# Expert 0's late tokens through DRAM, casts that give way, shorter routing, fillers at the seam and a new order in an attention + mixture-of-experts kernel

## The chip, the cores and the metric

One core of a Trainium2 chip runs one program. The metric is device microseconds of that core; the kernel before takes 403.33 us (median of 3 runs, 403.32 to 403.79).

## The reference

q, k, v, a_re and a_im are (4 batches, 8 heads, 768 steps, 48 dims). The first part is a gated linear recurrence with a complex decay, whose real part is read out by q:

```python
mag = np.sqrt(a_re * a_re + a_im * a_im)
scale = np.minimum(mag, 0.999) / (mag + 1e-06)
ar, ai = a_re * scale, a_im * scale
for t in range(S):
    S_re, S_im = (ar[t] * S_re - ai[t] * S_im + outer(k[t], v[t]),
                  ar[t] * S_im + ai[t] * S_re)
    y[t] = q[t] @ S_re
```

The second part takes y as x, 3072 tokens of 384. A token whose score `x @ w_skip` is not above 0 is copied. Any other token goes to the one of 8 experts that has the largest logit in `x @ w_gate`, and

```python
out = x + softmax_weight * (relu(x @ w1[e]) @ w2[e])      # w1: 384 x 1024, w2: 1024 x 384
```

All of it is float32.

## The kernel before, in words

**Units.** The attention is cut into 24 units: 6 chunks of 128 time steps (NCH) times 4 batches (B); unit u is chunk u // 4 of batch u % 4 and holds all 8 heads. `gates` computes a unit's decay (logs, exponentials, angles; ScalarE and VectorE, and two TensorE sums over time, `pt` and `pl`), `ready` loads q and k, multiplies them with the decay (`w`), transposes them on TensorE (`tp`, L437) and copies them out of PSUM on ScalarE (`wT`, L446). `unit` does the attention: `pa` (L478) and `py` (L520, L523) on TensorE work in 64-column halves, `yT` (L528, ScalarE) copies the result, and `px` (L537) turns it to token rows with the gate logits beside them. `lg` (L549, VectorE) sums the logits, `xa` (L553, ScalarE) copies the rows. Gates run in batches of units (STARTS), since ScalarE's tables for exponentials and for sines are loaded in turn.

**Routing.** For chunks 0 to 4, `route` works on four units at once: maximum of the logits, expert number, one-hot `oh`, a rank among the tokens of that expert (`rank`, bf16 matmuls), the softmax weight, a slot number. Then four indirect DMAs (`place`, L586, GpSimd queue) scatter the rows to a DRAM buffer `xs`, with 224 slots (CAP) for each expert. For the last chunk, `route1` (chain rt5_b and its second half re b) does the same unit by unit, b = 0 to 3.

**Expert 0 at the seam.** Expert 0 does not wait for the last four units' rows to go through DRAM. `early` (L583, SyncE queue) reads its slots once chunk 4's rows have landed, and for each of the last four units `spread` (L679) makes a 128 x 224 selection matrix `ohx`; the pieces `ga` (L883) then gather: 12 ordinary matmuls for each unit with its `ohx`, and 12 for the early rows with an identity matrix, in the order unit 20, 21, 22, early, 23, all summed in one PSUM tile. Copies of it (`xh`, L909, and the rest `xl`, L913) feed expert 0's first layer.

**Experts.** For each expert, `xg` (L891) loads its rows, `tx` (L903) transposes them, `ph` (L927) is layer 1 and `po` (L948 to L950) layer 2, each product in three float32r matmuls of high and low parts; `hh` and `hl` split the hidden values, `og` adds the weighted result, and `sc` scatters the rows to the output. The weights come in 7 pieces for each expert: `wd` (L843, SyncE queue), then a cast to the high part `wh` (L850, ScalarE, 0.8 to 1.1 us) and the low part `wl` (L855, VectorE, 0.9 to 1.2 us). Experts 0 and 1 are loaded and cast while the attention still runs.

**The order.** Every piece is handed to a planner (`Plan`) with an engine, an estimated time, a due time, what it needs and which buffers it takes. The planner runs a list schedule on these estimates: the engine that can start first takes, of the pieces that can start at that moment, the one with the smallest due time. SHIFT moves the due times of a kind of piece. The instructions are then issued on each engine in this order, and each engine works strictly through its own queue. So a piece whose inputs are later than the planner thought holds up everything behind it. Where the planner sees TensorE idle before the first `py`, it puts filler matmuls (`idle`, L755).

## Time and profile before

| what | us |
|---|---|
| median of 3 runs | 403.33 |
| profiled execution | 405.78 |
| its span, first to last instruction | 404.1 |
| TensorE busy in the span | 382.1 (95%) |
| VectorE busy | 318.0 (79%) |
| ScalarE busy | 278.8 (69%) |
| GpSimd busy | 68.8 (17%) |

The span is what the trace shows; the profiled execution adds 1.7 us around it. Busy time says what an engine had in flight, not that it was at its peak, and fillers count as busy. "Clock 1.00" is TensorE at its full 2.4 GHz, 0.50 is 1.2 GHz.

### The profile page before, as it was taken

The numbers are of one execution on the slowest core, as the hardware profiler recorded it, in microseconds if no ns is written. First come the engines' busy times: TensorE is split into PE (matmuls) and PEld (weight loads), VectorE is DVE, ScalarE is ACT, GpSimd is POOL, SyncE is SP. The second block draws the span as 40 slices with busy tenths as digits, with TensorE's granted clock in tenths as the row PEclk, the third lists the DMA queues.
The fourth block names the chain that finished last, engine by engine and source line by source line (L and its number), as shares of the span: only waits on it lengthen the run. The fifth ranks groups of instructions, "written<-read, shape, count | busy, mean of one in ns | idle before, by whom it ended". The sixth has DMA issues, their size and how long they took to land. (4 is left out here: it accounts for less than half of the span.)

```text
span 404.1 us, 9935 instructions
## 1 busy us (share of the span) xinstructions
PE 382.1 (95%) x3768; PEld 345.5 (86%) x3768; DVE 318.0 (79%) x728; ACT 278.8 (69%) x546; POOL 68.8 (17%) x102
## 2 busy tenths in 40 slices
PE   7888999999999999999998998899999999999992
PEld 7577788789888789889877988799999999999992
DVE  5679999999999999999978879858765777757220
ACT  5897989999998999698785574445454755546110
POOL 9100000034005100400540033102111110110101
PEclk9999999999999999999999899899999999999997
DMA  9958979789798688454625785596777868771001
GB/s 157 194 100 156 186 120 285 178 194 196 136 159 207 133 173 186 108 109 117 128 93 142 193 233 172 177 317 215 224 227 222 235 191 236 226 222 38 27 2 34
DMA packets 160758, 67.15 MB, mean 166 GB/s; under 512 B 142310, under 2 KB 156295, under 8 KB 160704
## 3 DMA queue, kind: packets, MB, share of 16 engines
q1 hardware_dynamic: 158144, 61.81, 64.8%
q0 software_dynamic: 2560, 4.63, 3.5%
q8 instruction: 32, 0.52, 0.5%
q14 instruction: 22, 0.18, 0.2%
HBM read 54.24 MB, written 14.98 MB: 171 GB/s over the span
## 5 line engine op out<-in xcount | busy, mean ns | idle before, releaser
L850 ACT CAST h<-r 128x768 fp32r<-128x768 f32 (+1 forms) x56 | 50.9, 928 | 36.3 <-PE po L950 20.4
L586 POOL DMA_INDIRECT xs<-xa,sl x24 | 35.8, 1493 | 206.7 <-ACT ain L261 75.4
L855 DVE TENSOR_TENSOR l<-r,h 128x768 fp32r<-128x768 f32 (+1 forms) x56 | 59.2, 1070 | 11.0 <-ACT h L850 11.0
L446 ACT COPY wT<-tp 96x512 f32<-96x512 f32 x92 | 50.3, 582 | 7.1 <-PE tp L437 7.1
L437 PE MATMUL tp<-ident,w 128*96 128x128 f32 x384 | 53.2, 278 | 1.9 <-DVE w L429 0.6
L927 PE MATMUL ph<-xh,h 128*128 128x224 f32 x192 | 53.7, 283 | 1.2 <-ACT xh L909 0.9
L927 PE MATMUL ph<-xh,l 128*128 128x224 f32 x192 | 52.9, 279 | 0.0
L927 PE MATMUL ph<-xl,h 128*128 128x224 f32 x192 | 50.6, 277 | 0.0
L437 PEld LDWEIGHTS tp<-ident,w 128*96 128x96 f32 x384 | 41.6, 128 | 8.3 <-issue 2.4
L933 ACT ACTIVATE hh<-ph 128x224 fp32r<-128x224 f32 x64 | 22.8, 359 | 34.8 <-PE ph L927 34.7
L429 DVE TENSOR_TENSOR w<-qk,cs 128x768 f32<-128x768 f32 x48 | 44.5, 949 | 0.2
L948 PE MATMUL po<-h,hh 128*112 128x384 f32 x128 | 43.5, 340 | 0.0
L950 PE MATMUL po<-h,hl 128*112 128x384 f32 x128 | 43.1, 337 | 0.0
L949 PE MATMUL po<-l,hh 128*112 128x384 f32 x128 | 43.1, 337 | 0.0
L478 PE MATMUL pa<-wT,wT 96*64 96x128 f32 (+1 forms) x768 | 38.2, 250 | 2.4 <-ACT wT L446 1.9
L927 PEld LDWEIGHTS ph<-xh,h 128*128 128x128 f32 x192 | 37.5, 195 | 1.8 <-ACT xh L909 1.0
L927 PEld LDWEIGHTS ph<-xh,l 128*128 128x128 f32 x192 | 37.7, 196 | 0.0
L520 PE MATMUL py<-at,vt 128*64 128x128 f32 x192 | 36.5, 279 | 1.1 <-DVE at L485 0.7
L478 PEld LDWEIGHTS pa<-wT,wT 96*64 96x64 f32 x768 | 33.7, 137 | 4.0 <-ACT wT L446 2.3
L937 DVE SCALAR_TENSOR_TENSOR hl<-ph,hh 128x224 fp32r<-128x224 f32 x64 | 23.6, 385 | 17.1 <-ACT hh L933 17.1
L520 PE MATMUL py<-at,vs 128*64 128x128 f32 x192 | 36.5, 279 | 0.0
L927 PEld LDWEIGHTS ph<-xl,h 128*128 128x128 f32 x192 | 36.1, 195 | 0.0
(170 smaller groups left out, 852.2 us busy)
## 6 DMA issues: line engine op xcount, KB each, us to landing
r<-in_moe_w_dram SPq DMA_DIRECT2D x24, 512.0 KB, 5.0
r<-in_moe_w_dram SPq DMA_DIRECT2D x32, 384.0 KB, 5.5
ain<-in_a_re_dram SPq DMA_DIRECT2D x24, 192.0 KB, 3.5
ain<-in_a_im_dram SPq DMA_DIRECT2D x24, 192.0 KB, 4.5
qk<-in_q_dram SPq DMA_DIRECT2D x24, 192.0 KB, 4.1
qk<-in_k_dram SPq DMA_DIRECT2D x24, 192.0 KB, 4.1
vt<-in_v_dram SPq DMA_DIRECT2D x24, 192.0 KB, 4.1
out_dram<-xa SPq DMA_DIRECT2D x5, 768.0 KB, 4.1
```

Source lines behind the costliest of these rows:

```text
L429: V.tensor_tensor(n, X["qk", u][:, k].unsqueeze(2).to_broadcast([128, H, 2, D]), X["cs", c][:, b], ALU.mult)
L437: nc.tensor.transpose(tp[:, h], n[:, hh * 4 + h].rearrange("p k d -> p (k d)"), self.ident)
L446: (V.tensor_copy if onV else A.copy)(X["wT", u, k][:, hh * 4:hh * 4 + 4], X["tp", u, k, hh])
L478: PE.matmul(pa[p, i, t0:], k[:, h, ts], q[:, h, t0:], start=True, stop=True)
L520: PE.matmul(py[j * 64:j * 64 + 64, hp], vs[:, hp] if j else vt[:, 2 * hp], at[:, 2 * hp + j], start=True, stop=(c == 0))
L586: self.nc.gpsimd.indirect_dma_start(out=self.xsv[c * B + b], out_offset=bass.IndirectOffsetOnAxis(ap=sl, axis=0), in_=xa[:, b], in_offset= ...
L850: nc.scalar.copy(X["W", e, n][0][:, ks], X["raw", e, i])
L855: nc.vector.tensor_tensor(lo[:, ks], X["raw", e, i], hi[:, ks], ALU.subtract)
L927: PE.matmul(ph, w[:, k, ks(j)], x[:, k], start=(i == 0), stop=(i == len(terms) - 1))
L948: PE.matmul(po, hh[:, j, ts(t)], w2h[:, j], start=(j == 0), stop=False)
L949: PE.matmul(po, hh[:, j, ts(t)], w2l[:, j], start=False, stop=False)
L950: PE.matmul(po, hl[:, j, ts(t)], w2h[:, j], start=False, stop=(j == NF - 1))
```

## The change

- The pieces `ga` of units 20 and 21 are gone (EARLY = 2). Their rows for expert 0 go through `xs` like all others; `early` now reads after the placements of these two units, and only units 22 and 23 get an `ohx`. The order is early, 22, 23, and the early rows are turned in transpose mode.
- The placements of units 22 and 23 wait for `early`.
- In the planner, where the piece chosen is a weight cast, any other piece of that engine that can start less than 0.71 us later (LOOK) goes first. The last cast of expert 1 comes after expert 0's input (HOLD).
- Routing: one step makes the expert number and the skip mark together (a skipped token gets an expert number of -8192, which puts its slot out of bounds); the small sum constant 1e-9 lives in a ninth column of a shared tile; the overflow mark is written straight to `todo`. `route` goes from 19 + 3 VectorE instructions to 13 + 2, `route1` from 10 + 9 pieces to 8 + 5 (units 20, 21), 10 + 5 (22) or 9 + 5 (23). The experts' regions of `xs` are in reverse order, with expert 0's last.
- Fillers are also put in where the planner sees TensorE idle between the last `yT` and the first `ph`. The first `ph` comes after the last decay factors (`f3`) and after the last rank sum.
- New planner constants: batches of gates (the last starts at unit 22, not 21), leads, SHIFT, a cost for each turn between half-width and full-width matmuls (TURN), and FINE, which moves single pieces; many `po` pieces are moved 10 to 20 units later, that is behind any other piece that can start.

```diff
-STARTS = [0, 3, 7, 11, 14, 18, 21]
-AHEAD, TRIG, READY, PULL = 3.0, 2.98, 1.66, 2.83
+STARTS = [0, 3, 7, 11, 14, 18, 22]
+AHEAD, TRIG, READY, PULL = 3.0, 3.08, 1.72, 2.49
-WAFTER, WGAP, CHECK = 5.0, 2.02, 3
-FETCH = 2.75
+WAFTER, WGAP, CHECK = 4.65, -0.13, 3
+FETCH = 2.87
+EARLY, HOLD, LOOK = 2, 6, 0.71
+FINE = {
...
+}
-LEADS = {0: 6.57, 1: 7.36, 2: 2.93, 3: 1.62, 4: 2.78, 5: 0.77, 6: 1.2, 7: 4.57}
+LEADS = {0: 7.24, 1: 6.22, 2: 3.18, 3: 1.87, 4: 3.38, 5: 0.58, 6: 0.38, 7: 3.19}
...
+            if key[0] in ("wh", "wl"):
+                s, at, key = min([x for x in l if x[0] < s + LOOK and x[2][0] not in ("wh", "wl")] or [(s, at, key)], key=lambda x: (x[0], str(x[2])))
-            if e == "P" and n > 0 and ("py", 0, 0) not in end:
+            if e == "P" and n > 0 and (("py", 0, 0) not in end or ("yT", B * NCH - 1) in end and ("ph", 0, 0) not in end):
...
-        self.nc.sync.dma_start(self.xe, self.xs[0:CAP, 0:DM].rearrange("(t p) d -> p t d", p=HALF))
+        self.nc.sync.dma_start(self.xe, self.xs[E * CAP:(E + 1) * CAP, 0:DM].rearrange("(t p) d -> p t d", p=HALF))
...
         steps = [
             ("V", 0.15, first),
-            ("V", 0.22, lambda: V.scalar_tensor_tensor(R["cand"], R["L"], R["mx"], iota, ALU.is_equal, ALU.mult)),
-            ("V", 0.15, lambda: V.tensor_scalar(R["act"], R["lg"][:, E:], 0.0, None, ALU.is_gt)),
+            ("V", 0.22, lambda: V.scalar_tensor_tensor(R["cand"][:, 0:E], R["L"], R["mx"], iota, ALU.is_equal, ALU.mult)),
+            ("V", 0.15, lambda: V.tensor_scalar(R["cand"][:, E:], R["lg"][:, E:], 0.0, -OFF, ALU.is_le, ALU.mult)),
             ("V", 0.15, lambda: V.tensor_reduce(R["am"], R["cand"], AX.X, ALU.min)),
-            ("V", 0.22, lambda: V.scalar_tensor_tensor(R["oh"], iota, R["am"], R["act"].to_broadcast([128, E]), ALU.is_equal, ALU.mult)),
+            ("V", 0.16, lambda: V.tensor_scalar(R["oh"], iota, R["am"], None, ALU.is_equal)),
             ("P", 0.15, rank),
...
-            ("V", 0.22, lambda: V.scalar_tensor_tensor(R["val"], R["oh"][:, 0:1], -BIG, R["pr"][:, 0:1], ALU.mult, ALU.add)),
+            ("V", 0.22, lambda: V.scalar_tensor_tensor(R["val"][:, 0:1], R["oh"][:, 0:1], -BIG, R["pr"][:, 0:1], ALU.mult, ALU.add)),
             ("V", 0.35, spread),
+        ] * (b >= EARLY) + [
+            ("V", 0.22, lambda: V.tensor_tensor_reduce(R["val"], R["oh"], R["pr"], 1.0, 0.0, ALU.mult, ALU.add, accum_out=R["rk"])),
+        ] + [("V", 0.15, sums)] * (b < B - 1)
...
-            self.plan.add(("early", 0), "S1", 1.1, at, [(f"rt{c - 1}", 19 + B)], take=[("xa", "early")])(self.early)
+            self.plan.add(("early", 0), "S1", 1.1, at + EARLY, [(f"rt{c - 1}", 14 + B)] + [(f"re{k}", 5) for k in range(EARLY)], take=[("xa", "early")])(self.early)
...
+            ("G1", 0.3, lambda: self.place(c, b, R["sl"], R["xa"]), ("xa", c * B + b), *[("early", 0)] * (b >= EARLY)),
...
-        for b in (0, 1, 2, -1, 3):
+        gas = [-1] + list(range(EARLY, B))
+        for i, b in enumerate(gas):
...
-                        PE.matmul(pts(0, t)[:, k], l, r, start=(b == 0 and k == 0), stop=True, skip_group_check=True)
+                        PE.matmul(pts(0, t)[:, k], l, r, start=(b < 0 and k == 0), stop=True, is_transpose=b < 0, skip_group_check=True)
...
-                     [(None, ("ph", e, j - 1))] * (j > 0) + [("at", u, 1), ("yT", u)] * (e == 0),
+                     [(None, ("ph", e, j - 1))] * (j > 0) + [("at", u, 1), ("yT", u), ("f3", c), (f"rt{c}_{B - 1}", 10)] * (e == 0),
```

## Rows read from the trace of the kernel before

**Rows 1.** Stretches of the span: us, each engine busy, TensorE clock, DMA share, GB/s.
```profile
0.00:36.00 36.00, 29.59 (x224) 25.40 (x224) 24.23 (x50) 27.89 (x52) 10.47 (x49) 1.00 0.94 149
36.00:218.00 182.00, 178.27 (x2100) 150.85 (x2102) 174.57 (x398) 165.15 (x331) 30.39 (x21) 1.00 0.73 156
...
246.00:258.37 12.37, 9.66 (x85) 8.70 (x85) 11.00 (x60) 5.11 (x12) 5.21 (x4) 1.00 0.56 159
258.37:396.90 138.53, 138.16 (x1003) 136.69 (x1003) 85.05 (x151) 63.71 (x123) 17.78 (x23) 0.99 0.59 179
396.90:404.10 7.20, 0.00 (x0) 0.00 (x0) 0.62 (x1) 0.00 (x0) 0.94 (x1) 0.68 0.08 23
```

**Rows 2.** Two shorter stretches, same columns.
```profile
221.00:227.00 6.00, 6.00 (x52) 5.51 (x54) 5.17 (x10) 3.36 (x7) 0.00 (x0) 0.72 0.73 179
259.00:264.00 5.00, 5.00 (x33) 5.00 (x31) 4.59 (x11) 1.96 (x5) 0.00 (x0) 0.66 0.65 194
```

**Rows 3.** TensorE timeline: start, us, line, out<-in, count, idle before and releaser.
```profile
218.73 0.88 PE L478 MATMUL pa<-wT,wT 96*64 96x64 f32 x16
220.95 0.93 PE L478 MATMUL pa<-wT,wT 96*64 96x128 f32 x16 [1.34 <-ACT wT L446]
```

**Rows 4.** ScalarE timeline, the same place.
```profile
219.37 1.04 ACT L850 CAST h<-r 128x1024 fp32r<-128x1024 f32 x1 [1.82 <-DMA r<-in_moe_w_dram]
220.32 0.57 ACT L446 COPY wT<-tp 96x512 f32<-96x512 f32 x1
```

**Rows 5.** TensorE timeline, from the last attention piece to the first expert.
```profile
245.61 0.39 PE L523 MATMUL py<-wT,st 96*64 96x128 f32 x4
...
247.69 1.16 PE L537 MATMUL px<-wg,yT 128*128 128x128 f32 x8
...
248.74 1.57 PE L883 MATMUL pt<-ohx,xa 128*128 128x112 f32 x12
...
255.02 1.56 PE L883 MATMUL pt<-early,xa 128*128 128x112 f32 x12 [0.20 <-DVE ohs L682]
...
258.37 0.37 PE L927 MATMUL ph<-xh,h 128*128 128x224 f32 x1 [0.87 <-ACT xh L909]
```

**Rows 6.** ScalarE timeline, the same stretch.
```profile
246.11 1.05 ACT L850 CAST h<-r 128x1024 fp32r<-128x1024 f32 x1 [1.25 <-DMA r<-in_moe_w_dram]
247.06 0.58 ACT L528 COPY yT<-py 128x512 f32<-128x512 f32 x1
...
257.54 0.78 ACT L909 CAST xh<-pt 128x336 fp32r<-128x336 f32 x2 [0.44 <-PE pf L402]
```

**Rows 7.** VectorE timeline, the same stretch.
```profile
243.65 0.33 DVE L679 TENSOR_SCALAR ohx<-iotac,m 128x224 f32<-128x224 bf16 x1
...
249.42 1.22 DVE L855 TENSOR_TENSOR l<-r,h 128x1024 fp32r<-128x1024 f32 x1
250.56 0.19 DVE L549 TENSOR_REDUCE lgs<-px 128x9 f32<-128x36 f32 x1
...
252.27 0.16 DVE L671 TENSOR_REDUCE m<-lgs 128x1 f32<-128x8 f32 x1
...
253.06 1.24 DVE L855 TENSOR_TENSOR l<-r,h 128x1024 fp32r<-128x1024 f32 x1
...
254.54 0.34 DVE L679 TENSOR_SCALAR early<-iotac,m 128x224 f32<-128x224 bf16 x1
```

**Rows 8.** GpSimd timeline, placement of unit 21.
```profile
250.20 1.28 POOL L586 DMA_INDIRECT xs<-xa,sl  x1 [2.20 <-DVE todo L720]
```

**Rows 9.** SyncE queue, the early read.
```profile
240.53 0.33 SPq L583 DMA_DIRECT2D early<-xs  x1
```

**Rows 10.** DMA issues: median us to landing.
```profile
xs<-xa,sl POOLq DMA_INDIRECT x24, 3.9
```

**Rows 11.** TensorE timeline, a transposing piece of expert 1.
```profile
268.66 0.74 PE L903 MATMUL pt<-ident,xg 112*128 112x112 f32 x6
```

More of the change, by code (lines that the diff above doesn't have):

```diff
@@ L112, in order @@
                 if r is not None:
-                    can.setdefault(e, []).append((max(r, free[e]) + 0.1 * (e == "P" and mode != (key[0] in self.HALVES)), self.ops[key][2], key))
+                    can.setdefault(e, []).append((max(r, free[e]) + self.TURN[mode] * (e == "P" and mode != (key[0] in self.HALVES)), self.ops[key][2], key))
             assert can, sorted(todo, key=str)[:9]
@@ L468, in unit @@
         for hh in range(2):
-            @add(("pa", u, hh), "P", 0.69, t, [("wT", u, k, hh) for k in range(2)], take=[("pa", u, hh)], free=[("wT1", u)])
+            @add(("pa", u, hh), "P", 0.68, t, [("wT", u, k, hh) for k in range(2)], take=[(f"pa{hh}", u)], free=[("wT1", u)])
             def _(hh=hh):
@@ L509, in unit @@
         for hh in range(2):
-            @add(("py", u, hh), "P", 0.90 if c else 0.45, t,
+            @add(("py", u, hh), "P", 0.88 if c else 0.44, t,
                  [("at", u, hh), ("lv", u)] + ([("Sb", u), ("wT", u, 0, hh)] if c else []),
@@ L530, in unit @@
         bank = ("c" if late else "g", "px", u)
-        @add(("px", u), "P", 0.925, t, [("yT", u), ("wg", 0)], take=[bank], free=[("yT", u)])
+        @add(("px", u), "P", 0.91, t, [("yT", u), ("wg", 0)], take=[bank], free=[("yT", u)])
         def _():
@@ L642, in route @@
         if c == 0:
-            for i in range(20, 20 + B):
+            for i in range(15, 15 + B):
                 steps[i] += (("zero", 4),)
         else:
-            steps[0] += ((f"ro{c - 1}", 2),)
+            steps[0] += ((f"ro{c - 1}", 1),)
         done = [
-            ("V", 0.22, lambda: V.scalar_tensor_tensor(self.todo[:, :, c], R["ov"], 1.0 / BIG, R["act"], ALU.mult, ALU.mult)),
             ("V", 0.26, lambda: V.tensor_reduce(R["cnt"], R["oh"].rearrange("p b e -> p e b"), AX.X, ALU.add)),
@@ L702, in route1 @@
-        self.plan.ops[name, 9][3].append(("early", 0))
-        self.plan.rel.setdefault(("g", name), []).append((name, 10))
+            self.plan.add(("early", 0), "S1", 1.1, at + EARLY, [(f"rt{c - 1}", 14 + B)] + [(f"re{k}", 5) for k in range(EARLY)], take=[("xa", "early")])(self.early)
+        self.chain(name, at, steps, ("lg", c * B + b), *([(f"rt{c}_{b - 1}", 9 + 2 * (b > EARLY))] if b else [(f"ro{c - 1}", 1)]))
+        self.plan.rel.setdefault(("g", name), []).append((name, n))
         self.plan.ops[name, 5][4].append(("g", name))
@@ L750, in idle @@
     def idle(self, n):
-        if "warm" not in self.x:
-            self.x["warm"] = self.ps_y.tile([128, H // 2, C], F32, name="warm", tag="py")
+        if "yof" in self.x and ("yT", B * NCH - 1) not in self.x:
+            return
+        name = "hold" if "yof" in self.x else "warm"
+        if name not in self.x:
+            self.x[name] = self.ps_y.tile([128, H // 2, C], F32, name=name, tag="py")
         for i in range(n):
-            self.nc.tensor.matmul(self.x["warm"][:, 0], self.turns, self.turns, start=True, stop=True)
+            self.nc.tensor.matmul(self.x[name][:, 0], self.turns, self.turns, start=True, stop=True)
     def emit(self, which):
@@ L835, in weights @@
             ks = slice(k * st, k * st + st)
-            old = [] if e < 2 else [("ph", e - 2, NF - 1)] if i < KD else [("po", e - 2, 1, NF - 1)]
+            old = [] if e < 2 else [("ph", e - 2, NF - 1)] if i < KD else [("po", e - 2, t, NF - 1) for t in range(2)]
             @add(("wd", e, i), "S1", 1.5 if i < KD else 1.15, t + gap * i, list(need) + ([(None, ("wd", e, i - 1) if i else ("wd", e - 1, 6))] if e or i else []), take=[(raw_, e, i)])
@@ L843, in _ @@
                 nc.sync.dma_start(raw, w[e].rearrange("(k p) f -> p k f", p=128)[:, ks])
-            @add(("wh", e, i), "A", 1.05 if i < KD else 0.835, t + gap * (i + 0.4), [("wd", e, i)] + old)
+            @add(("wh", e, i), "A", 1.05 if i < KD else 0.835, t + gap * (i + 0.4), [("wd", e, i)] + old + [(None, ("wh", e, i - 1))] * (i > 0) + [("xl", 0, 1)] * (e == 1 and i >= HOLD))
             def _(i=i, k=k, n=n, m=m, ks=ks):
@@ L872, in pts @@
             return X["pts", e, t]
-        for b in (0, 1, 2, -1, 3):
+        gas = [-1] + list(range(EARLY, B))
+        for i, b in enumerate(gas):
             need = [("early", 0)] if b < 0 else [(f"rt{c}_{b}", 9), ("xa", c * B + b)]
-            last = {0: wTs, 1: [("ga", 0)], 2: [("ga", 1)], -1: [("ga", 2)], 3: [("ga", -1)]}[b]
-            @add(("ga", b), "P", 1.36, n - 0.5 if b < 3 else n + 0.2, need + last, take=[("mpt", 0, 0), ("mpt", 0, 1)])
+            last = [("ga", gas[i - 1])] if i else wTs
+            @add(("ga", b), "P", 0.62 if b < 0 else 1.45, n - 0.5 if b < 3 else n + 0.2, need + last, take=[("mpt", 0, 0), ("mpt", 0, 1)])
             def _(b=b):
@@ L1007, in check @@
             ("V", 0.2, flag),
-        ], ("f3", NCH - 1), ("px", B * NCH - 1), *[(f"re{b}", 9) for b in range(B)])
+        ], ("f3", NCH - 1), ("px", B * NCH - 1), *[(f"re{b}", 5) for b in range(B)])
         self.plan.ops["ck", 10][4].append(("mpo", "ck"))
```

126 lines of the change are left out of this document (69 added, 57 removed), and 26 rows, old and new, of the table FINE.

## The prediction

> **What bounds the kernel now.** I read the windows first, then the timelines of single engines where TensorE is not full. The profiled execution takes 405.78 us, its span 404.1 us; 1.7 us lie around it. In the expert part TensorE is busy 138.16 of 138.53 us, and VectorE and ScalarE only 85 and 64 us [rows 1]: that part is the length of its matmuls, all of which stay. The 7.20 us behind the last matmul are two scatters and the end of the program, and stay too. In the middle of the attention (36 to 218 us) TensorE is busy 178.27 of 182 us and VectorE 174.57: two engines at their end, 3.7 us to win at most without less matmul work. In the first 36 us TensorE is idle for 6.4 us, and much of its busy time is fillers; the first units' gates on ScalarE and VectorE set the pace there.
>
> What can be won lies in three places. First, the seam between attention and experts, 246.00 to 258.37 us, where TensorE is idle for 2.7 us [rows 1] and spends time on gathers. Second, two falls of the clock: in the 6 us from 221 the mean granted clock is 0.72, in the 5 us from 259 it is 0.66 [rows 2]; TensorE was busy throughout, so 6 x 0.28 = 1.7 and 5 x 0.34 = 1.7 us went to 1.2 GHz. Both follow a gap of TensorE. Third, the first of those gaps itself: 1.34 us in which `pa` waited for `wT` [rows 3]. ScalarE shows why: a weight cast stood ahead of that copy and waited 1.82 us for its DMA [rows 4].
>
> **The change part by part.**
>
> *The seam.* The last matmul of unit 23's `py` ends at 245.61 + 0.39 = 246.00 [rows 5]. Its copy `yT` came only at 247.06, behind a cast that ran from 246.11 for 1.05 us [rows 6], and `px` at 247.69. With the cast giving way, `yT` starts at 246.0, and `px` at about 246.65, ending at 247.8 instead of 248.85 (−1.04). The logit sum then came at 250.56, behind a cast of 1.22 us and routing steps of unit 21; the maximum came at 252.27, behind routing steps of unit 22; five steps took 252.27 to 253.06; the next cast, 1.24 us, stood ahead of the last two steps; the selection ended at 254.54 + 0.34 = 254.88 [rows 7]. Without the casts, with lg at 247.85: 0.2 for the sum, 0 to 0.8 for what is left of unit 22 (up to five steps of 0.16), 0.8 for five steps, 0.8 for rank and the last two (0.58 from the end of the cast to the end of the selection, and the rank matmul). That ends at 249.6 to 250.4. The last gather is 1.57 us and from the start of `xh` to the first `ph` it is 258.37 − 257.54 = 0.83 [rows 5, 6]: first `ph` at 252.0 to 252.8 by VectorE's chain.
>
> TensorE has its own sum. Two of five gathers go, 2 x 1.57 = 3.1 us. Three stay. An early gather of 12 transposes takes at most twice the 0.74 us of six [rows 11], 1.5 us; the other two 1.57 each; 4.6 together. If all three come behind `px`, they end at 247.8 + 4.6 = 252.4, and `ph` starts at about 253.3. I take 253.4, **−5.0 us**. The small matmuls of rank and decay factors fall into waits. The ends: 252.0 (−6.4), if the early gather is done before `px`; and no gain or a loss, if the early rows come late, which is the first rival.
>
> The Trainium skill ("DMA: Bandwidth & Descriptors", section on the anatomy of one SWDGE DMA) fits a DMA of GpSimd's queue as about 2.0 us plus its bytes at 436 GB/s. As an estimate by that page, the 198 KB of one placement would land in 2.5 us; this trace has a median of 3.9 us for the 24 of them, and the trace is what I use. By the page's figure the last time allowed for unit 21's placement would be 1.4 us later than below.
>
> *The wait that is added.* The early read needed chunk 4's placements before; it was issued at 240.53 [rows 9], and the first `ohx`, which shares what it frees and waits for it, ran at 243.65 [rows 7]: at most 3.1 us. Now it also needs unit 21's placement, which takes 3.9 us to land [rows 10]. For the early gather to start at 247.8, unit 21 must be placed by 247.8 − 3.1 − 3.9 − 0.4 (issue) = 240.4. Before it was placed at 250.20 [rows 8], but its routing stood behind unit 20's `ohx`, hence behind the early read, and that link is cut. On SyncE's queue the weight loads of experts 0 and 1 stand behind the early read; on GpSimd's queue the placements of units 22 and 23 do, and expert 1's rows behind those. Expert 1's input is needed only when expert 0's layer 1 ends, one eighth of 138.5 = 17 us after the first `ph` for the whole expert, so 5 us of delay there are covered. If that cover goes, each further us is a us.
>
> *Clock at the start of the experts.* TensorE's idle time ahead of it is filled by fillers and shortened. I take the whole **−1.7** [rows 2]; ends 0 and −1.7. A filler that is issued when its gap turns out not to exist costs its own length, for which I add nothing: the gap that it stands for was waited out anyway.
>
> *Casts that give way.* At 219 the loss is 1.34 + 1.7 = 3.0 us [rows 2, 3]. The new rule looks at the planner's times, and the cast stood there because its load landed later than planned, which the rule doesn't see. Yet the copy behind it is let ahead when it is ready within 0.71 us. I take half, **−1.5**; ends −3.0 and 0. The price of giving way is a later cast; 14 casts (7 for each expert) lie here, and of expert 0 only three are needed for its first `ph`.
>
> *Shorter routing.* VectorE saves 7 instructions in each of five `route` calls and 4 to 6 in each `route1`. At 0.16 us a step [rows 7] that is 35 x 0.16 = 5.6 us in `route`, beside a TensorE that idles 3.7 us in 182. Together with the new order in the middle I take **−0.5**; ends −3.7 (no idle left) and +3.0 (one more stall like that at 219, with its fall of clock).
>
> *Start, experts, end:* 0. The start is bounded by gates that don't change in number; their order does. Ends ±2, a third of the 6.4 us idle there. In the experts `po` is put behind all else that is ready; TensorE has 0.4 us idle to lose, and the other engines 40% room.
>
> Sum: −5.0 − 1.7 − 1.5 − 0.5 = −8.7 us. The profiled execution becomes 405.78 − 8.7 = 397.1 (span 395.4), the median 403.33 − 8.7 = **394.6 us**.
>
> **The rivals.**
>
> *The two DRAM trips become the seam (slower).* If unit 21 is still placed at 250.20, the early rows land at 250.2 + 0.4 + 3.9 + 3.1 = 257.6, three gathers end at 262.2, and `ph` starts at 263.0, 4.7 later than before. With the cast and order terms (−2.0) and no clock gain that is 403.33 + 4.7 − 2.0 = 406.0. It turns the sign from a placement at about 247.6 on. For it: the due times put a unit's second half behind much, and that placement came 13 us behind unit 21's logits here. Against: what held it is cut. 8%.
>
> *Half of the seam.* Unit 21 placed at 243: `ph` starts 2.5 later than forecast, and the stall at 219 or one like it stays (+1.5): 398.6. 15%.
>
> *The clock falls all the same.* After fillers and gathers comes a pause for `xh`, and the clock falls in the first `ph` as before: 394.6 + 1.7 = 396.3. The fall at 259 came behind 2.7 us of idle spread over 12 us [rows 1, 2], so shorter pauses might do it too. The Trainium skill ("TensorE: Matmul & The Clock Gate", Part 4, on PE-mode transpose) says that a matmul in transpose mode does not count as busy in the same way for the clock; the early gather is now of that kind, and no row here isolates it. 12%.
>
> *More than forecast.* The stall at 219 goes whole (−1.5), `ph` starts at 252.0 (−1.4), the start gives 1: 390.7. 12%.
>
> *No net change.* The rest of the new order brings three stalls of 3.0 us each: about 403. Two falls of clock in 404 us say that such stalls are rare with these estimates. 3%.
>
> **How the numbers follow.** Forecast 50%, 394.6. The range 390.0 to 400.5 takes in the half seam, the clock and most of "more"; it leaves out the slower rival, no change and a tail, some 14%. This kernel's runs tell 0.2% (0.8 us) from no change. Faster: 50 + 15 + 12 + 12 = 89%. Same: 3%. Slower: 8%.
>
> **What would show it.** Right: the first `ph` at 253 to 254 if the stretch before it keeps its time; three groups of 12 gathers; in ScalarE's timeline `yT` of unit 23 right behind `py`; a clock of 1.00 from 250 to 270; the idle time of `pa` for `wT` under 0.7; about 138 us from the first `ph` to the last matmul, 7.2 behind it. Wrong: gathers waiting for the early read; any window with a clock of 0.5 in the middle; the first `py` later than at 36; `ph` of expert 1 waiting for rows or casts.

## The result, and the profile after

The changed kernel takes 407.82 us (median of 20 runs, 403.24 to 415.57), the kernel before, timed beside it, 404.31 us (20 runs, 403.06 to 406.39): a ratio of 1.0071 (95% interval 1.0048 to 1.0094, given in brackets from here on). The ratio is one of means and leaves out the changed kernel's three longest runs (409.93 us and more), each over 1.5% above its shortest. So it is slower by 0.7%, where 2.2% less was forecast. Its runs also spread over 12 us, those of before over 3.3.

The profiled execution takes 407.59 us. Windows cut at the first `py`, the end of the last `py`, the first `ph` and the end of the last matmul (us, then PE, PEld, DVE, ACT, POOL busy, TensorE clock, DMA share, GB/s; the last line is a shorter stretch):

```profile
0.00:40.19 40.19, 32.72 (x223) 28.64 (x223) 24.61 (x51) 28.59 (x52) 10.26 (x50) 0.92 0.99 154
40.19:244.68 204.49, 201.81 (x2452) 172.82 (x2452) 190.72 (x437) 178.02 (x357) 31.27 (x27) 1.00 0.74 154
244.68:253.73 9.05, 6.90 (x63) 6.07 (x63) 7.95 (x39) 4.27 (x10) 1.94 (x2) 1.00 0.61 188
253.73:398.93 145.20, 138.95 (x1003) 136.11 (x1003) 90.55 (x156) 68.71 (x128) 18.87 (x23) 0.99 0.59 189
398.93:405.90 6.97, 0.00 (x0) 0.00 (x0) 0.62 (x1) 0.00 (x0) 0.94 (x1) 0.85 0.16 42
...
350.00:360.00 10.00, 8.37 (x45) 8.20 (x46) 3.74 (x6) 3.01 (x5) 0.19 (x1) 0.83 0.55 174
```

Against [rows 1, 5] (the last matmul of before ends at 396.88 us; [rows 1] is cut at 396.90):

| stretch | before | after | difference | forecast |
|---|---|---|---|---|
| up to the end of the last `py` | 246.00 | 244.68 | −1.32 | −2.0 |
| from there to the first `ph` | 12.37 | 9.05 | −3.32 | −5.0 |
| first `ph` to last matmul | 138.51 | 145.20 | +6.69 | −1.7 |
| behind it | 7.22 | 6.97 | −0.25 | 0 |
| sum (span) | 404.1 | 405.9 | +1.8 | −8.7 |

The first two terms have the sign and most of the size, the first in part by luck: it is +3.74 us up to the first `py` (40.19 against 36.45, forecast 0) and −5.06 from there on (forecast −2.0). The third is the error. In it TensorE is idle for 145.20 − 138.95 = 6.25 us, against 0.35 before. Its timeline there (start, us, line, out<-in; in brackets the idle time ahead of it and what ended that) shows four waits that make 5.4 of the 6.25:

```profile
258.18 0.37 PE L977 MATMUL ph<-xh,h 128*128 128x224 f32 x1 [1.18 <-DVE hl L987]
...
262.44 0.51 PE L953 MATMUL pt<-ident,xg 112*128 112x112 f32 x3 [1.19 <-DMA xg<-xs]
...
293.17 0.51 PE L953 MATMUL pt<-ident,xg 112*128 112x112 f32 x3 [1.14 <-DMA xg<-xs]
...
351.63 0.77 PE L953 MATMUL pt<-ident,xg 112*128 112x112 f32 x6 [1.89 <-DMA xg<-xs]
```

Three of them are waits of `tx` for `xg`, the rows of an expert. Behind the last one the clock falls: 0.83 over 350 to 360. Why the rows of the later two come late stands on SyncE's queue. First the kernel before, then the changed one (issues of `xg`; there are 8, the first three at once, the fourth and the last shown; the last line is TensorE's first transposes of the last expert's rows):

```profile
260.74 1.34 SPq L891 DMA_DIRECT2D xg<-xs  x3
280.45 0.42 SPq L891 DMA_DIRECT2D xg<-xs  x1
...
349.54 0.37 SPq L891 DMA_DIRECT2D xg<-xs  x1
...
366.24 0.45 PE L903 MATMUL pt<-ident,xg 112*128 112x112 f32 x3
```

```profile
255.94 1.33 SPq L941 DMA_DIRECT2D xg<-xs  x3
286.94 0.42 SPq L941 DMA_DIRECT2D xg<-xs  x1
...
366.65 0.38 SPq L941 DMA_DIRECT2D xg<-xs  x1
...
371.32 0.77 PE L953 MATMUL pt<-ident,xg 112*128 112x112 f32 x6
```

The first group is issued 4.8 us earlier than before, as the first `ph` is; expert 3's rows are asked for 6.5 us later, expert 7's 17.1 us later. From that last issue to the transposes there were 16.7 us, and there are 4.7. For experts 3 to 7 this lead was 16.7 to 17.4 us and is 4.7 to 8.1, while a load of `xg` takes 4.1 to 8.0 us to land (median 5.2, after). `xg` has three buffers, and in the program a buffer is free only when `og` and the scatter of the third expert before are done. These need the `po` pieces, which the change moves back. The wait at 262.44 is another case: expert 1's rows belong to the first group and wait for no buffer, but with `po` moved back its transposes stand further ahead, 4.9 us behind the issue (255.94 to 260.80) where there were 7.9 (260.74 to 268.66, [rows 11]).

The same shows on VectorE: the last low cast of the weights, before and after.

```profile
368.58 0.95 DVE L855 TENSOR_TENSOR l<-r,h 128x768 fp32r<-128x768 f32 x1
```

```profile
389.28 0.95 DVE L904 TENSOR_TENSOR l<-r,h 128x768 fp32r<-128x768 f32 x1
```

It ended 27.4 us before the last matmul, and ends 8.7 us before it: in the program a weight tile of layer 2 is released by the last `po` of the second expert before, so a late `po` makes a late cast (without the moved `po` pieces, in e2_po below, it ended at 370.3, 25.4 us before the last matmul). So the new order has used up the slack with which loads were covered.

The start shows a loss of another kind. ScalarE waits for a row copy and then for unit 6's decay load, and VectorE does unit 6's gates ahead of unit 0's `at` (three timelines: ScalarE, VectorE, TensorE with its `pa` and the first `py`):

```profile
30.24 0.52 ACT L315 ACTIVATE tr<-ain 128x384 f32<-128x384 f32 x1 [2.12 <-DMA row<-tr]
...
34.83 0.52 ACT L315 ACTIVATE ain<-ain 128x384 f32<-128x384 f32 x1 [2.07 <-DMA ain<-in_a_re_dram]
...
35.94 0.56 DVE L348 TENSOR_TENSOR tr<-ain,tr 128x384 f32<-128x384 f32 x1 [1.61 <-ACT tr L315]
...
38.77 0.69 DVE L539 TENSOR_TENSOR at<-pa,masks 128x512 f32<-128x512 f32 x1
...
31.79 2.88 PE L532 MATMUL pa<-wT,wT 96*64 96x128 f32 x32 [1.90 <-ACT wT L500]
...
40.19 0.32 PE L574 MATMUL py<-at,vt 128*64 128x128 f32 x1
```

The first `py` comes 3.7 us later than before (36.45). Behind TensorE's wait of 1.90 us its clock is 0.50 from 32 to 38 us, which is why the first window has a mean of 0.92.

### The profile page after: what moved, and what is told of

It reads as the page before. It is cut to its first block, busy times and chain, and to the rows that moved or that the text cites. A ratio compares the mean times of both kernels' runs of the same rounds, so it can differ in the third digit from the quotient of the medians.

```text
span 405.9 us, 9810 instructions
## 1 busy us (share of the span) xinstructions
PE 380.4 (94%) x3738; PEld 343.6 (85%) x3738; DVE 314.4 (77%) x681; ACT 279.6 (69%) x546; POOL 63.3 (16%) x103
## 5 line engine op out<-in xcount | busy, mean ns | idle before, releaser
L637 POOL DMA_INDIRECT xs<-xa,sl x24 | 28.8, 1199 | 208.6 <-DMA row<-tr 77.4
L899 ACT CAST h<-r 128x768 fp32r<-128x768 f32 (+1 forms) x56 | 51.0, 928 | 13.2 <-DMA r<-in_moe_w_dram 10.3
L977 PE MATMUL ph<-xh,h 128*128 128x224 f32 x192 | 52.3, 277 | 2.5 <-DVE hl L987 1.6
L491 PE MATMUL tp<-ident,w 128*96 128x128 f32 x384 | 51.8, 274 | 0.6 <-DVE w L483 0.4
L977 PE MATMUL ph<-xh,l 128*128 128x224 f32 x192 | 51.8, 274 | 0.0
L532 PE MATMUL pa<-wT,wT 96*64 96x128 f32 (+1 forms) x768 | 40.8, 255 | 2.1 <-ACT wT L500 1.9
L532 PEld LDWEIGHTS pa<-wT,wT 96*64 96x64 f32 x768 | 35.0, 140 | 4.6 <-ACT wT L500 2.4
L977 PEld LDWEIGHTS ph<-xh,l 128*128 128x128 f32 x192 | 36.8, 192 | 0.0
```

The costliest lines, as they stand in the source:

```text
L491: nc.tensor.transpose(tp[:, h], n[:, hh * 4 + h].rearrange("p k d -> p (k d)"), self.ident)
L532: PE.matmul(pa[p, i, t0:], k[:, h, ts], q[:, h, t0:], start=True, stop=True)
L637: self.nc.gpsimd.indirect_dma_start(out=self.xsv[c * B + b], out_offset=bass.IndirectOffsetOnAxis(ap=sl, axis=0), in_=xa[:, b], in_offset= ...
L899: nc.scalar.copy(X["W", e, n][0][:, ks], X["raw", e, i])
L977: PE.matmul(ph, w[:, k, ks(j)], x[:, k], start=(i == 0), stop=(i == len(terms) - 1))
```

## The experiments

All are edits of the changed kernel unless said otherwise; each was timed beside runs of the kernel before on its chip. "Experts" is the time from the first `ph` to the end of the last matmul in the profiled execution, and "last `py`" the time at which it ends; both come from one execution of each kernel, so a difference of 1 or 2 us between two of them is not shown to be the edit's. The ratio to the kernel before is what decides on the time.

**1. Which edit costs the experts 6.7 us.** Four runs; before takes 404.75 us.

e2_po: `- 'po': {(0, 0, 1): 5.99, ...}` (the row of FINE, cut short here; it has 35 entries)

> The changed kernel with one edit: the single due times of the layer 2 pieces po (their row of FINE) are left out, so that an expert's layer 2 comes before the next expert's layer 1 again. Theory A (pushing po back delays og and the scatters, and with them the three buffers of xg, so that an expert's rows are loaded 6 us later and arrive after TensorE has run out of other work): the expert part, first ph to last matmul, shrinks from 145.2 to 138.5 to 140.5 us, TensorE waits for xg under 0.5 us in all, time about 402 against 407.8. Rival B (the weight loads, which all have nearly the same due time now, stand ahead on SyncE's queue and fill the DMA engines): expert part still 143 us or more, time 406 to 408.

405.11 us, ratio 1.0005 [0.9983, 1.0026]; experts 140.98, the waits for `xg` 0.38 in all, the fourth `xg` issue at 279.24, leads of 10.8 to 13.6 us for experts 3 to 7. This is theory A by its mechanism; its 138.5 to 140.5 us and 402 us were too good. The moved `po` pieces cost 4.2 us in the experts and about 0.7% of the whole.

e3_oldw: `- WAFTER, WGAP = 4.65, -0.13` / `+ 5.0, 2.02`

> The changed kernel with one edit: the due times of the weight pieces of experts 2 to 7 are as before (WAFTER 5.0, WGAP 2.02). Theory A (late xg because of po pushed back): expert part stays at 143 to 147 us with TensorE waits for xg of 2 us or more, time 406 to 409. Rival B (weight loads ahead of xg): expert part 138.5 to 140.5, time about 402.

408.45 us, 1.0103 [1.006, 1.0145]; experts 142.64, above rival B's 138.5 to 140.5 and just under theory A's 143 to 147; `tx` still waits four times for `xg`, 4.1 us together. As the ratio is no better than the changed kernel's, the weights' due times are not the cause.

e1_start: after the planner, `lv` of unit 1 and `lq` of unit 3 are moved behind `mv` of units 0 to 2 in the list

> The changed kernel with one edit: on SyncE's queue the loads of v for unit 1 and of q, k for unit 3 are issued after the three row copies (row<-tr of units 0 to 2) instead of before them. Theory A (the start is late because these row copies, on which the next units' gate buffers wait, are issued at 27.2 instead of 24.9 us, so that ScalarE waits 2.1 us for one and TensorE's clock falls behind that gap): row copies issued by about 24 us, no ScalarE wait over 1 us on them, no clock of 0.5 before 40 us, first py at 36.5 to 37.5 instead of 40.2, and 3 to 3.7 us less in all: about 404.3 against 407.8. Rival B (the start is late for another reason, the order of the gates on ScalarE and VectorE): first py stays at 39 to 40.5, time within 1 us of 407.8. The expert part stays at 144 to 147 us under both.

409.42 us, 1.0119 [1.0082, 1.0156]. The wait for the row copies went (`pa` waits 0.45 instead of 1.90 us), and the time did not: ScalarE then waited 3.45 us for unit 6's decay load, and the first `py` came at 39.54. So theory A, the row copies as the cause of the late start, fell.

e4_both: both edits

> The changed kernel with both edits, the row copies of units 0 to 2 first and po not pushed back. Theory A in both places: first py at 36.5 to 37.5, expert part 138.5 to 140.5, time 397.5 to 400, so that what the changed kernel won between them (8.4 us from the first py to the first ph) comes out. If the parts are not independent (the middle won only because the start was late and the queues had filled up): 401 to 404.

406.94 us, 1.0053 [1.0029, 1.0078]; first `py` 39.84, last `py` 246.67, experts 140.79, as in e2_po. Both times that were said (397.5 to 400, 401 to 404) were too good.

**2. The start, and the buffers.** Before takes 404.94 us.

e5_sp: `self.place_after((("la",6),("U",0)), (("lv",0),("wg",0)), (("lv",1),("mv",1)), (("lq",3),("mv",2)))`

> Edit: in the changed kernel, SyncE's queue in the start is put back into the order of before: the decay load of unit 6 (L279) ahead of the gate weights and unit 0's v, and the v load of unit 1 and the q/k load of unit 3 behind the three row copies of units 0 to 2. All other queues keep the new order. Theory (the start's loss of 3.7 us is this queue: the late load of unit 6 holds ScalarE for 2.1 to 3.5 us, and VectorE's gates of unit 6 stand ahead of the decay of unit 0): the first py comes at 36.5 to 37.5 instead of 40.2 and 39.5 in the two kernels tried, no wait of ScalarE of over 1 us near 35 us, and the kernel gains 2.5 to 3.5 us over the changed kernel: about 404.5 to 405.3. Rival A (the new order of ScalarE's and VectorE's gates sets the start, the waits for loads only show it): the waits go, and the first py stays at 39 to 40; 407 to 408.

408.15 us, 1.0064 [1.0033, 1.0094]. The mechanism of the theory held, its price did not: the first `py` is at 36.45 as before, and 65 us later the gain is given back, in the state update of unit 7:

```profile
36.45 0.29 PE L574 MATMUL py<-at,vt 128*64 128x128 f32 x1 [0.45 <-DVE at L539]
...
101.74 1.54 PE L553 MATMUL ps<-vt,w 128*96 128x64 f32 x16 [2.86 <-DMA vt<-in_v_dram]
```

The clock falls behind that wait (0.85 and 0.81 in the two windows of 5 us from 100), and the last `py` ends at 245.38, no earlier than with the late start (244.68). Rival A, the order of the gates, fell.

e6_la6: only `("la",6)` is moved behind `("U",0)`

> Edit: only the decay load of unit 6 is moved to its old place on SyncE's queue; the v load of unit 1 and the q/k load of unit 3 stay ahead of the row copies. Theory: ScalarE's wait for unit 6's load goes, the wait of 2 us for the row copies at 30 us stays, as it has only moved. First py at 37 to 38.5, about 405.5 to 406.5. Rival A: first py at 39 to 40. Rival B (the earlier load delays wg, v and q/k of units 0 to 2 on the queue, as it did before): pa waits longer than 1.9 us and the first py is no earlier.

409.11 us, 1.0108 [1.0069, 1.0147]; first `py` at 41.34: rival B. ScalarE waits longer for the row copies:

```profile
31.93 0.52 ACT L315 ACTIVATE tr<-ain 128x384 f32<-128x384 f32 x1 [3.74 <-DMA row<-tr]
```

Yet its last `py` ends at 245.33. With a first `py` anywhere from 36.4 to 41.3 the attention ended at 244 to 247 in these runs.

e7_comb: the edits of e5_sp and e2_po

> Edits: SyncE's start order of before, and the FINE row that moves 47 po pieces back is taken out. Theory: both losses are undone, the gain at the seam stays: first py 36.5 to 37.5, first ph 252 to 253, last matmul 393 to 394; about 401 to 402, faster than both kernels (ratio to before about 0.993). Rival A: the start stays at 39 to 40 and the time at that of the kernel without the po row, 405.1.

406.33 us, 1.0023 [0.9991, 1.0056]; first `py` at 36.31, unit 7's wait 3.91 us, last `py` 247.13, experts 141.35. The theory missed by over 4 us. Most of that is given back at 103 us, by this wait and a clock of 0.92 and 0.74 in the two windows of 5 us from 100.

e8_xg4: the edits of e5_sp, and `- xg=3` / `+ xg=4`; `po` stays moved

> Edits: SyncE's start order of before, and four buffers instead of three for the rows of an expert (xg and its index list); the po pieces stay moved back. Theory (the moved po pieces do harm only because an expert's rows wait for a buffer that the scatter of the third expert before holds): the waits of tx for xg of 1.1 to 1.9 us go, the expert part is 140 to 141 us instead of 145.2, and the time that of the kernel with both edits, 401 to 402. Rival (moving po back harms in itself, by the products that wait for hh/hl or by PSUM buffers): the expert part stays at 143 to 145 us though tx no longer waits; 404 to 405.

406.22 us, 1.0029 [1.0001, 1.0057]; experts 140.36 (TensorE idle 1.6 us) against 145.71 in e5_sp, which has one buffer less and is else the same; `tx` waits once, 0.58 us. Experts 4 to 6 have leads of 13.2 to 16.2 us again, expert 7 has 5.4. The theory holds for the expert part: with one buffer more the moved `po` pieces do nearly no harm in this profile. In the ratio the buffer gives 0.35%, which the two intervals don't set clear of nothing. The time is over 4 us above what was said; unit 7's wait is still there (2.83 us).

Taken together: the six profiles with the moved `po` pieces and three buffers (after, e1, e3, e5, e6, e9) have experts of 142.64 to 145.83 us, the five without the moved pieces, with a fourth buffer, or both (e2, e4, e7, e8, e10) 140.36 to 142.32. Of the two kernels below that add another edit to e10_all, e11_w06 has 144.81 and e12_early0 147.08.

**3. What gives the rest back.** Before takes 404.47 us.

e9_lv7: as e5_sp, and `(("lv",7),("py",4,0)), (("lq",10),("lv",7)), (("la",16),("lq",10))`

> Edits: SyncE's start order of before, and unit 7's v load moved ahead of unit 10's q/k load, unit 16's decay load and the factor copy that stood ahead of it, as early as its buffer allows (behind py of unit 4). The po pieces stay moved back, three xg buffers. Theory (the 3.7 us won at the start are given back at 102 us, where the state update ps of unit 7 waits for its v load on SyncE's queue, 2.9 us, and the clock falls behind it): the wait at 102 us goes, the clock stays at 1.00 there, first ph at 250 to 251 instead of 254.4; with an expert part of 145 the profile ends 3 to 4 us earlier than with the start order alone: about 404 to 405. Rival (SyncE's queue is late as a whole: q/k of unit 10 or the decay load of unit 16, now behind, hold the middle instead): another wait of 1 to 3 us between 95 and 125 us, first ph at 253 to 254.

406.98 us, 1.0064 [1.0037, 1.009]. The wait at 102 went, and others of 0.7 and 1.3 us came at 155 and 158 (again `wT` and a v load); first `ph` 253.43, experts 143.74. The rival, 35 us later than it said.

e10_all: e9_lv7, e2_po and four `xg` buffers

> Edits: as the run with unit 7's v load moved (both queue edits), and also without the po row of FINE and with four xg buffers. Theory: start 36.4, middle 214 to 215, experts 139.5 to 140.5: the last matmul ends at 390 to 391, about 398 to 400 us, 1 to 1.5% faster than before. Rival (rest of the expert loss is the wait of ph for hl at 259 with a fall of the clock, which neither edit touches): expert part 141 and 400 to 402. If SyncE's queue takes the gain at the start back again: 403 to 404.

405.07 us, 1.0022 [1.0002, 1.0042]; experts 142.32, with waits of 1.24 for `hl`, 1.45 for `xg` and 1.57 for `xh`. No gain over e2_po: theory and rival fell, and 405.07 is above the 403 to 404 of the third reading as well.

e11_w06: e10_all, and `wh`, `wl` of expert 0's piece 6 behind its fourth `hh`, `hl`

> Edits: as the run before, and the last cast pair of expert 0's weights (wh and wl of piece 6) is moved behind the fourth hh and hl of expert 0. In the changed kernel both stand ahead of the first hl, and wait for a load that is issued only at 252.2. Theory (the rest of the loss in the experts, some 2 us, is the wait of the fourth ph for hl, 1.2 to 2.9 us, and the clock of 0.66 that follows): the wait of ph for hl near 259 is under 0.3 us, no window of the clock below 0.95 in 255 to 265, expert part 1 to 2.5 us shorter than in the run before it. Rival (hl waits for VectorE's checks and hh as such, not for the cast): wait and clock stay, no difference.

406.61 us, 1.0025 [0.9992, 1.0058]. The wait for `hl` at 258 went, but the clock fell in that place all the same, with TensorE busy for the whole window:

```profile
255.00:260.00 5.00, 5.00 (x32) 5.00 (x31) 3.22 (x13) 1.77 (x4) 0.00 (x0) 0.66 0.68 225
```

And e10_all, which has this wait (1.24 us at 257.72), has a clock of 1.00 from 250 to 268. So the wait doesn't make that fall. Experts 144.81, longer and not shorter: theory and rival both fell.

e12_early0: e10_all with `EARLY = 0` (five groups of gathers)

> Edits: as the run with both queue edits, no po row and four xg buffers, and EARLY = 0: no unit of the last four goes to expert 0 through DRAM, so five groups of 12 gathers stand at the seam again, and the early read waits for chunk 4's placements only. Theory (the two gathers that go are 3.1 us of TensorE on the path): last py to first ph 2 to 3.5 us longer than in the kernel with three gathers, the time 2 to 3 us longer. Rival (the gathers lay in waits for routing all the same, the gain at the seam came from the casts that give way): no difference above 1 us.

411.1 us, 1.0189 [1.0162, 1.0215]. From the last `py` to the first `ph`:

```profile
242.37:255.33 12.96, 9.35 (x84) 8.52 (x85) 8.63 (x38) 5.96 (x12) 2.92 (x3) 1.00 0.52 156
```

That is 3.9 us more than 9.05, where 2 to 3.5 was said; against e10_all the time is 6 us longer, where 2 to 3 was said. So the two units through DRAM are worth up to 3.9 us at the seam in this order. It isn't pure, as the planner, given other pieces, also made another order of the rest (the last `py` ends at 242.37, experts 147.08).

**4. The planner's constants for the experts.** These four ran on a slower chip, on which the kernel before takes 412.7 us (17 runs, 409.05 to 419.01); only their ratios are compared, and their profiles with each other.

e13_plan: FINE rows of `po`, `ph`, `tx` and one entry of `wl` out; SHIFT of `idx tx ph hh hl po og wh` out; WAFTER, WGAP as before; `if key[0] in ("wh", "wl") and key[1] < 2`

> Edits: the changed kernel, its attention and seam untouched, with the expert part planned as before: no FINE rows for po, ph and tx, no SHIFT entries for idx, tx, ph, hh, hl, po, og and wh, weights due as before (WAFTER 5.0, WGAP 2.02), casts of experts 2 to 7 do not give way. The issued order then has a layer 1 every 17.2 us as before and an expert's rows are asked for 16 us ahead of their transposes. Theory (the order of the experts' pieces is the whole loss of 6.7 us there): expert part 138.5 to 139.5 us, first ph at 253.7 to 255, time 400 to 401.5, 0.8 to 1.1% faster than before. Rival (the seam hands its gain on: rows of the last units, weights and casts come later, so the experts start into waits and a fall of the clock): expert part 140.5 to 142 us, 402.5 to 405.

419.2 us, 1.0168 [1.0081, 1.0256]; no wait for `xg`, but five waits for `hl`, 5.7 us in all. Its profile is of the longest of its six runs (423.25 us), so its experts, 147.16, are not compared. e14_plan_sp: the same with the queue edits of e9_lv7

> Edits: as the run before, and SyncE's queue order of before in the start with unit 7's v load moved ahead. Theory (the first py at 36.4 instead of 40 is worth little, as TensorE does other units' pieces meanwhile and the last py of the attention came at 244.2 to 245.4 in the runs with that start, at 244.7 to 247.0 in those without): last py at 244 to 245, the time within 1.5 us of the run before, 399.5 to 401. Rival (start counts in full once the experts keep their time): 397 to 398.

415.91 us, 1.0086 [1.0041, 1.0132]; experts 143.89, no wait for `xg`, four waits for `hl`, 4.7 us. The theory of e13_plan fell, in both: order as before is not enough. Whether the start is worth anything here these two can't say, as their intervals overlap.

e15_look0: e13_plan with `LOOK = 0.0`

> Edits: as the first of these runs, and LOOK = 0: weight casts no longer give way to pieces that are ready soon. All else, the two units through DRAM and the shorter routing included, stays. Theory (the casts are part of the gain at the seam and of the 3.0 us at 219): copies of unit 23 wait behind a cast again, from last py to first ph 10.5 to 13 us instead of 9.05, first ph at 256.5 to 259, time 403 to 406. Rival (the two gathers less are all of the gain): 9 to 10 us, first ph at 254 to 255, time as in the first of these runs.

418.9 us, 1.0171 [1.0098, 1.0245]. From the last `py` to the first `ph` 17.1 us, above the theory's 10.5 to 13 and above the 12.36 of e16_bexp, which has the old seam on the same chip; then comes the best expert part of all, 137.05 us. Casts that hold their place cost the seam 8 us here, and the experts take 6.8 us less than in e14_plan_sp. In the whole they make no difference against e13_plan (1.0171 and 1.0168). So three groups of gathers alone don't shorten the seam here: without the rule for casts it is longer than the old one with five.

e16_bexp: the kernel before with the rows `po`, `ph`, `tx` of FINE and the eight SHIFT entries

> Edits: the kernel before, its attention and seam untouched, with the changed kernel's FINE rows for po, ph and tx and its SHIFT entries for idx, tx, ph, hh, hl, po, og and wh; weights due as before. Theory (the order alone costs 4 to 7 us, whatever the seam does): expert part 142.5 to 145.5 us, tx waiting for xg by over 1 us at one or more experts, time 407.5 to 411. Rival (the order does harm only behind the new seam): expert part 138.5 to 140, time 404 to 406.

426.65 us, 1.0352 [1.0267, 1.0437]. TensorE's clock and idle time in the experts:

```profile
262.60:413.45 150.85, 143.07 (x1003) 140.57 (x1003) 83.89 (x151) 62.98 (x123) 22.83 (x23) 0.95 0.52 164
```

`tx` waits 2.21 and 1.37 us for `xg`, `po` 3.61 us for `og`. The order does its harm behind the old seam too, which is the theory; the size, 3.5% of the time, was above the 4 to 7 us that it said.

**5. The rule for casts.** Before takes 404.77 us.

e17_look1: e14_plan_sp with `key[1] < 1`

> Edits: the changed kernel with the expert part planned as before (no FINE rows for po, ph, tx; no SHIFT entries for idx, tx, ph, hh, hl, po, og, wh; weights due as before), casts give way for expert 0 only, and SyncE's order of the start as before with unit 7's v load ahead. Theory (late casts and the order of the expert pieces are the loss in the experts, the seam is not): from last py to first ph 9.05 us, expert part 138.5 to 140.5 us, time 0.5 to 1% less than before on the same chip. Rival (the seam hands its gain on, casts of expert 1 come late in any case): expert part 141 to 143 us, within 0.3% of before.

404.57 us, 0.9996 [0.9965, 1.0026]; last `py` 242.79, seam 9.05, experts 144.97. The rival by the time, though the mechanism is another: casts that hold their place wait on ScalarE for loads, `hh` stands behind them, and `ph` waits for `hl`. SyncE, ScalarE, VectorE, TensorE:

```profile
280.92 15.78 SPq L897 DMA_DIRECT2D r<-in_moe_w_dram  x9
...
294.01 1.04 ACT L904 CAST h<-r 128x1024 fp32r<-128x1024 f32 x1 [1.55 <-DMA r<-in_moe_w_dram]
294.96 0.60 ACT L988 ACTIVATE hh<-ph 128x224 fp32r<-128x224 f32 x2
...
295.08 1.22 DVE L909 TENSOR_TENSOR l<-r,h 128x1024 fp32r<-128x1024 f32 x1 [1.37 <-ACT h L904]
...
296.67 0.37 PE L982 MATMUL ph<-xh,h 128*128 128x224 f32 x1 [2.33 <-DVE hl L992]
```

e18_blook: the kernel before, and nothing but these two lines

```diff
+            if key[0] in ("wh", "wl"):
+                s, at, key = min([x for x in l if x[0] < s + 0.71 and x[2][0] not in ("wh", "wl")] or [(s, at, key)], key=lambda x: (x[0], str(x[2])))
```

> Edits: the kernel before, with one thing added: a weight cast gives way to any other piece of its engine that can start less than 0.71 us later. Theory (the rule alone lets the casts fall behind): the last low cast of the experts' weights ends less than 20 us before the last matmul instead of 27.4 us in some experts or comes behind their first layer in the first three experts; expert part 139.5 to 142 us with waits of ph for hl or of po for weights; attention and seam 0 to 3 us shorter; time within 0.5% of before. Rival (casts have slack enough, the rule is a gain without a price): expert part 138.5 us, time 0.4 to 0.8% less than before.

401.85 us, ratio **0.9897 [0.9857, 0.9937]**: faster than both kernels, and the best of all that ran. (Six runs; the quotient of the medians is 0.993, so the gain is 0.7 to 1.0%.) Its windows, cut as above:

```profile
36.45:242.59 206.14, 202.62 (x2457) 173.18 (x2458) 194.52 (x466) 179.32 (x358) 35.42 (x25) 1.00 0.73 159
242.59:253.20 10.61, 9.26 (x85) 8.63 (x85) 10.11 (x62) 4.21 (x10) 3.66 (x4) 1.00 0.73 212
253.20:393.33 140.13, 138.39 (x1003) 136.61 (x1003) 88.95 (x152) 68.40 (x127) 20.66 (x24) 0.99 0.61 190
...
219.00:225.00 6.00, 6.00 (x87) 5.61 (x85) 5.54 (x15) 4.27 (x8) 0.00 (x0) 1.00 0.93 192
```

Against [rows 1 to 3]: attention −3.4 us (the wait of 1.34 and the clock of 0.72 near 220 are gone), seam −1.8, experts +1.6. Expert 3's rows are asked for at 275.69, expert 7's at 346.11, and the last low cast ends 26.7 us before the last matmul. So the rule alone doesn't make the last casts late, and the theory fell there; the order of `po` does. What the rule costs is at the start of the experts: `ph` waits 0.89 us for `xl`, and 0.8 for `hl`.

```profile
255.01 0.60 PE L929 MATMUL ph<-xl,h 128*128 128x224 f32 x3 [0.89 <-DVE xl L915]
```

The clock is 0.66 from 255 to 260, but such a fall is in the kernel before as well [rows 2].

## Why the prediction was wrong, step by step

**The step that failed: "Start, experts, end: 0", with its reason "In the experts `po` is put behind all else that is ready; TensorE has 0.4 us idle to lose, and the other engines 40% room."** Busy shares were taken for slack. What covered the experts was neither TensorE's idle time nor room on VectorE, but how far ahead a buffer came free: three `xg` buffers, released through `po`, `og` and the scatter. Moving `po` back leaves the matmuls as they are and takes that lead away, from 16.7 us to 4.7. The term measured +6.7 us where 0 was forecast (and −1.7 for the clock). e2_po (the row out, 140.98 against 145.20) and e8_xg4 (a fourth buffer, 140.36 against 145.71) take 4.2 and 5.4 us away, and e16_bexp brings the loss to the kernel before. "`ph` of expert 1 waiting for rows" was named as a sign of being wrong, but no term had it, and the nearest rival, "No net change" (three stalls from the new order, 3%), named neither the experts nor a buffer.

The rest of the expert part, some 2 us against 138.51, is not settled to the last step. It is enough to use up the seam: against before, e2_po has its last `py` 0.3 us earlier, a seam 3.3 us shorter and experts 2.5 us longer, and its time is level (1.0005). Waits for `hl` or `xl` behind the first `ph` appear in e18_blook too, where the rule for casts is the only edit (TensorE idle 1.7 us in the experts, 0.35 before); e15_look0, without that rule, has 137.05, but behind a seam that is 8 us longer and gives the casts that much more time. So that part most likely goes with casts that were put off; it is not shown. e11_w06 moved one such cast pair and gained nothing, so which cast it is stays open.

**The seam: −5.0 forecast, −3.3 measured.** The mechanism was right: `yT` right behind `py` (the last `py` ends at 244.68), three groups of gathers, clock 1.00. The sum was short by 1.7 us, as the timelines show (one line of ScalarE, then TensorE):

```profile
244.76 0.59 ACT L582 COPY yT<-py 128x512 f32<-128x512 f32 x1 [0.51 <-PE py L577]
...
244.60 2.05 PE L591 MATMUL px<-wg,yT 128*128 128x128 f32 x16
...
247.68 0.79 PE L933 MATMUL pt<-ident,early 112*128 112x112 f32 x6
248.98 0.17 PE L721 MATMUL pr<-oh,tri 128*128 128x8 bf16 x1 [0.50 <-DVE todo L761]
...
249.03 2.91 PE L933 MATMUL pt<-ohx,xa 128*128 128x112 f32 x24
...
252.51 0.35 PE L456 MATMUL pf<-gT,twice 48*96 48x32 f32 x2 [0.27 <-ACT gT L451]
253.73 0.37 PE L977 MATMUL ph<-xh,h 128*128 128x224 f32 x1 [0.87 <-ACT xh L959]
```

The early gather was cheaper than thought (0.79, not 1.5): in transpose mode it is six matmuls of 112 x 112, not twelve. The other two groups took 2.91, not 3.1. But the early gather starts 1.0 us behind `px`, as its rows had not landed:

```profile
241.06 0.97 POOL L637 DMA_INDIRECT xs<-xa,sl  x1 [1.32 <-issue]
...
244.04 0.33 SPq L634 DMA_DIRECT2D early<-xs  x1
```

Unit 21 was placed at 241.06, 0.7 us behind the time that the prediction set as the limit, with an attention that ended 1.3 us earlier; the early read was issued at 244.04 and took 3.6 us to land, to 247.64. Then 0.5 us of waiting with a rank product, and 1.8 us from the last gather to `ph`, where 0.9 was counted: the decay factors (`pg`, `pf`) stand ahead of `xh`, and "fall into waits" was wrong for them. That the first `ph` came at 253.73 where 253.4 was said is luck: these errors were cancelled by a shorter attention. And the gain rests on the rule for casts as much as on the gathers (e15_look0).

**Casts that give way: −1.5 forecast.** Mis-sized: the stall and the fall of the clock at 219 went whole in e18_blook, 3.4 us up to the last `py`, and the rule alone is 1.0% [0.6, 1.4] of the time. It is the only part that a run shows to be a gain by itself.

**Start, clock, routing.** The start was priced at 0, ends ±2, as "bounded by gates that don't change in number"; the first `py` came 3.7 us late, and e5_sp shows that the order of loads on SyncE's queue did it. What that costs at the end of the attention is not shown: with the old order of the start the last `py` ended at 242.59 (e18_blook) and 242.79 (e17_look1), against 244.68, but these two differ in more than the start, and e5_sp and e9_lv7, with waits for v loads later on, end at 245.38 and 244.38. The clock gain of 1.7 us behind the seam came true in the profile after, and a fall of 1.7 us at 351 to 356 (clock 0.67) took its place. The shorter routing and the fillers at the seam were not tried by themselves, nor the two DRAM trips on the kernel before. The routing was also counted wrongly: `route` has 18 + 3 VectorE instructions in the kernel before, not 19 + 3, so it saves 6 in each call, and 30 x 0.16 = 4.8 us, not 5.6; no term hangs on it.

**The noise.** The three runs of before that were known lay within 0.5 us; twenty of them span 3.3 us with a median of 404.31. So "0.2% from no change" was too fine, though the miss is far larger.

**The rivals.** None came true. "Two DRAM trips" (the slower one) has with 406.0 the time nearest to the measured one, but for a reason that did not occur: unit 21 was placed at 241.06, not 250.20, and the seam got shorter. "The clock falls all the same" was a real effect: of the 13 profiles with the seam of 9.05 us on the faster chips, 8 show it between 250 and 265, and 5, the changed kernel's own among them, do not. As a reason the prediction drew on the Trainium skill ("TensorE: Matmul & The Clock Gate", Part 4), by which a matmul in transpose mode does not count as busy in the same way. The kernel before [rows 2] and e18_blook have the fall (0.66) with the early gather as ordinary matmuls, so transposes there are not needed for it. No run isolates them.

## What to carry to other kernels

Before an edit that only reorders is priced at zero, list for each load which buffer it waits for and which instruction frees that, and measure the lead from its issue to its first use against the time that it takes to land: that lead, not the busy share, is what a later free buffer eats. A wait taken away early in a long pipeline can be given back at the next late load on the same queue: here a first `py` that was 3.7 us earlier (36.45) was worth nothing behind the wait at 101.74. Try the parts of a bundled change one at a time: here two lines gave 0.7 to 1.0%, and the changed kernel, which has the same rule for casts among its parts, came out 0.7% slower than without any of them.

## What the runs showed of the hardware

- Of the five chips of the experiments, one ran the kernel before 2% slower (412.7 us against 404.5 to 404.9). On it `tp` waited 3.1 and 3.2 us for `wT` near 220 us and `px` 2.6 us for `yT` at 244 and 248 us (e14_plan_sp, e13_plan); the 13 kernels with the seam of 9.05 us on the other chips have no wait of TensorE over 0.9 us from 205 us to their first `ph`. No row here shows what makes it slower.
- The clock fell to a mean of 0.66 over 5 us in which TensorE was busy for 5.00 us (e11_w06, 255 to 260 us), right behind a seam of 9.05 us with 2.4 us idle; in other kernels with the same seam it did not (the changed kernel: 1.00 from 250 to 270, with 2.2 us idle in the seam).
- Six transposes of 112 x 112 in transpose mode took 0.79 us (above, at 247.68), where the 12 ordinary matmuls that they replace took 1.57 in the kernel before, both at a clock of 1.00:

```profile
253.25 1.57 PE L883 MATMUL pt<-ident,early 112*128 112x112 f32 x12
```
